# Feeding the first four tiles of a fused attention and MLP kernel in another order: loads on two queues, statistics and norms reordered

## The chip, the cores and the metric

The kernel runs on one core of a Trainium2 chip. The metric is the device time of one execution in microseconds (us). A profile gives the span of one execution, which is about 2 us shorter than its time. Engines are called as in the profile: PE multiplies matrices, PEld is its weight load, DVE is the vector engine, ACT the scalar engine, POOL the general one, SP the one that only issues transfers.

Kernels are compared over five rounds in which the kernel before and the new one run on the same chip.

## The reference, cut to what matters

```python
xn  = layernorm(x)                                # x: 2048 rows of 640, bf16
q, k, v = split(xn @ wqkv)                        # 32 heads of 20
o   = linear_attention(phi(q), phi(k), v) @ wo    # phi = elu + 1
out = x + o + (gelu(xn @ w1 + b1) @ w2 + b2)      # F = 1536
```

The rows are cut into 16 tiles of 128 rows. Tiles 0 to 3 are group 0, tiles 4 to 7 group 1, and so on. Everything begins with four tiles of x: statistics on DVE, the reciprocal root ("rstd") on ACT, the norm on DVE, a transpose on PE, a copy from PSUM to SBUF, and then the product with K's weights.

## The kernel before

PE needs, in this order, tile 0 (only centred, its scale is applied later), then normed tiles 1, 2 and 3. These are the loads and the start of the program, with cuts marked:

```python
load_x(0, 1)                    # SP's queue; 160 KB each tile
load_x(1, 2)
load_x(2, 4)                    # tiles 2 and 3 in one transfer

def emit_later_loads():         # called after the statistics of tile 1
    nc.vector.memset(w1[:, 0, 0:1], 0.0)       # holds w1 back until DVE is there
    nc.sync.dma_start(out=w1[:, :, 0 : F // 2], ...)
    load_x(4, 8)                # group 1
    ...                         # b1, second half of w1, Q's weights, x of groups 2 and 3

nc.vector.memset(wqk[:, 0, D : D + TOK], 0.0)  # holds wk back by 0.27 us
load_wk(0, 3)                   # ACT's queue: K's weights, chunks 0 to 2 (480 KB)
load_wk(3, NC)                  # chunks 3 and 4 (320 KB)
...
emit_stats(0); emit_center(0); emit_T_first(0, ...)      # T: transposes on PE, copies on ACT
emit_warm(1)                    # L190: a matmul of constants, its result isn't used
emit_stats(1)
emit_later_loads()
emit_stats_half(2, 0)
emit_rstd(0, 2)
emit_norm(1)
emit_stats_half(2, 1)
emit_Ka(0, 0, 3)                # first K product, chunks 0 to 2
emit_T_first(1, ((0, 3, nc.scalar.copy),))
emit_rstd(2, 3)
emit_T_first(1, ((3, NC, nc.scalar.copy),))
emit_stats(3)
emit_norm(2)
emit_Ka(0, 3, NC); emit_Kb(0)
emit_Ka(1, 0, 3)
emit_T(2, ...)
emit_rstd(3, 4); emit_norm(3); emit_norm(0)
...                             # K of tiles 1 to 3, then the MLP's first product, L485
```

Of the kernel before, what the change touches and what calls it, by code (L numbers as in the profile page):

```python
# [15 lines left out]
def kernel(  # L16
# [12 lines left out]
    nc = tc.nc  # L29
# [4 lines left out]
    S, D = x2d.shape  # L34
# [4 lines left out]
    NC = D // P  # L39
    NJ = F // P  # L40
    TOK = 512
# [34 lines left out]
    wqk = early.tile([P, NC, 2 * D], BF16, name="wqk", tag="early")  # L76
# [24 lines left out]
    def bank(dtype=F32, hold=False):  # L101
        n = turn.pop(0)
        if isinstance(hold, str):
            named[hold] = n
        else:
            (held if hold else turn).append(n)
        return psum.tile([P, TOK if dtype == F32 else 2 * TOK], dtype, name=f"bank{n}", tag=f"bank{n}")
# [16 lines left out]
    def load_x(t0, t1, queue=nc.sync):  # L124
        queue.dma_start(out=x_all[:, t0:t1, :], in_=xv[:, t0:t1, :])

    def load_wk(k0, k1):
        nc.scalar.dma_start(out=wqk[:, k0:k1, D : 2 * D], in_=wqkv_v[:, k0:k1, D : 2 * D])

    load_x(0, 1)  # L130
    load_x(1, 2)
    load_x(2, 4)

    def emit_later_loads():
        nc.vector.memset(w1[:, 0, 0:1], 0.0)
        nc.sync.dma_start(out=w1[:, :, 0 : F // 2], in_=w1_v[:, :, 0 : F // 2])
        load_x(4, 8)
        nc.sync.dma_start(out=b1_bf[:], in_=B_b1.rearrange("(j p) -> p j", p=P))
        nc.sync.dma_start(out=w1[:, :, F // 2 : F], in_=w1_v[:, :, F // 2 : F])
        nc.sync.dma_start(out=wqk[:, :, 0:D], in_=wqkv_v[:, :, 0:D])  # L140
        load_x(8, 12)
        load_x(12, 16)

    nc.vector.memset(eps_t[:], EPS)
    nc.vector.memset(neg_half[:], -0.5)
    nc.vector.memset(wqk[:, 0, D : D + TOK], 0.0)
    load_wk(0, 3)
    load_wk(3, NC)
    make_identity(nc, identity)

    def emit_masks():
# [45 lines left out]
    def emit_stats_half(t, half):  # L197
        if half == 0:
            stats_of[t] = small.tile([P, 2, nc.vector.BN_STATS_DIM], F32, name="stats")
        st = stats_of[t]  # L200
        nc.vector.bn_stats(out=st[:, half, :], in_=x_all[:, t, half * HALF : (half + 1) * HALF])  # L201
        if half == 1:
            nc.vector.bn_aggr(out=mv[:, t, :], in_=st[:])

    def emit_stats(t):
        emit_stats_half(t, 0)
        emit_stats_half(t, 1)

    def emit_rstd(t0, t1):
        r = rstd[:, t0:t1]  # L210
        nc.scalar.activation(out=r, in_=mv[:, t0:t1, 1], func=ACT.Ln, bias=eps_t[:], scale=1.0)
        nc.scalar.activation(out=r, in_=r, func=ACT.Exp, scale=-0.5)
# [6 lines left out]
    def emit_norm(t, c0=0, c1=NC):  # L219
        ds = slice(c0 * P, c1 * P)  # L220
        nc.vector.tensor_scalar(  # L221
            out=xn[:, t, ds], in0=x_all[:, t, ds], scalar1=mv[:, t, 0:1], scalar2=rstd[:, t : t + 1],
            op0=ALU.subtract, op1=ALU.mult,
        )
# [6 lines left out]
    def emit_T(t, copy, splits=(0, NC)):  # L231
        pT = bank(BF16)[:, 0:D].rearrange("p (c n) -> p c n", n=P)
        for c in range(NC):
            nc.tensor.transpose(pT[:, c, :], xn[:, t, c * P : (c + 1) * P], identity[:])
        for c0, c1 in zip(splits, splits[1:]):
            copy(out=xnT[:, c0:c1, t * P : (t + 1) * P], in_=pT[:, c0:c1, :])
# [15 lines left out]
    def emit_T_first(t, parts):  # L252
        for c0, c1, copy in parts:
            pT = bank()[:, 0 : (c1 - c0) * P].rearrange("p (c n) -> p c n", n=P)
            for c in range(c0, c1):
                nc.tensor.matmul(
                    pT[:, c - c0, :], lhsT=xn[:, t, c * P : (c + 1) * P], rhs=identity[:],
                    start=True, stop=True,
                )
            copy(out=xnT[:, c0:c1, t * P : (t + 1) * P], in_=pT)  # L260
# [45 lines left out]
    def emit_Ka(t, k0=0, k1=NC):  # L306
        if k0 == 0:
            K_ps[t] = bank(hold="first" if t == 0 else t < TPG)
        for k in range(k0, k1):
            nc.tensor.matmul(  # L310
                K_ps[t][:], lhsT=xnT[:, k, t * P : (t + 1) * P], rhs=wqk[:, k, D : D + TOK],
                start=(k == 0), stop=(k == NC - 1),
            )

    def emit_Kb(t):
        g, i = divmod(t, TPG)
        if i == 0:
            rest_ps[g] = bank(hold=True)
        for k in range(NC):
            nc.tensor.matmul(  # L320
                rest_ps[g][:, i * REST : (i + 1) * REST],
                lhsT=xnT[:, k, t * P : (t + 1) * P], rhs=wqk[:, k, D + TOK : 2 * D],
                start=(i == 0 and k == 0), stop=(k == NC - 1), skip_group_check=True,
            )
# [173 lines left out]
    emit_warm(1)  # L498
    emit_stats(1)
    emit_later_loads()  # L500
    emit_stats_half(2, 0)
    emit_rstd(0, 2)
    emit_norm(1)
    emit_stats_half(2, 1)
    emit_Ka(0, 0, 3)
    emit_T_first(1, ((0, 3, nc.scalar.copy),))
    emit_rstd(2, 3)
    emit_T_first(1, ((3, NC, nc.scalar.copy),))
    emit_stats(3)
    emit_norm(2)  # L510
    emit_Ka(0, 3, NC)
    emit_Kb(0)
    emit_Ka(1, 0, 3)
    emit_T(2, nc.vector.tensor_copy, (0, 3, NC))
    emit_rstd(3, 4)
    emit_norm(3)
    emit_norm(0)
# [426 lines left out]
    class Pair:  # L944
# [63 lines left out]
        def copy(self, name):  # L1008
            self.open(name)
            nc.scalar.copy(out=self.ps[name], in_=self.ps["a"])  # L1010
# [219 lines left out]
```

## Time and profile before

| | before |
|---|---|
| time, median of 6 (range) | 197.59 us (197.46 to 197.94) |
| span of the profile | 195.4 us |
| PE busy | 98% of the span |
| statistics of tile 0 start (x0 has landed) | 3.07 us |
| DVE then idle for x2 and x3 | 0.94 us |
| norm 1, norm 2 start | 7.03, 9.01 us |
| first matmul of the MLP | 13.74 us |

From the page of the profile: the span, each engine's busy time with its share, and the shares of the chain of work that ended last.

```profile
span 195.4 us, 3381 instructions
...
PE 190.8 (98%) x1260; PEld 111.8 (57%) x1260; DVE 163.6 (84%) x393; ACT 89.6 (46%) x165; POOL 21.1 (11%) x52
...
PE 93%; DMA 2%; DVE 2%; SPq 0%; issue 0%
```

The chain that ended last, in order of time; columns are start, duration and what ran. "DMA" is a transfer waited for.

```profile
1.72 4.88 DMA x_all<-in_A_x_dram
...
7.03 0.43 DVE xn L221
...
9.10 0.32 DVE xn L221
9.46 0.45 PE bank_201 L234 x5
...
13.90 1.08 PE bank_268 L485 x5
...
192.20 0.29 DVE late L1003
```

The chain runs through the joint load of x2 and x3 (4.88 us from 1.72 to its landing; DVE stood idle for the last 0.94 us of it), then DVE's norms of tiles 1 and 2, then PE alone; the last line is the last DVE addition. From the chain's first matmul of the MLP to that addition everything is PE work until the last few microseconds. So the head, up to about 13.7 us, is where this change can act. (PE's 98% count matmuls of constants too: until 5.27 us most of what PE does is those, L190.)

The timeline of the head (start, duration, engine, line, operation; in brackets the idle time before it and what ended it):

```profile
3.07 0.89 DVE L201 BATCH_NORM_STATS2 stats<-x_all 128x6 f32<-128x320 bf16 x2 [1.81 <-DMA x_all<-in_A_x_dram]
...
6.62 0.49 DVE L201 BATCH_NORM_STATS2 stats<-x_all 128x6 f32<-128x320 bf16 x1 [0.94 <-DMA x_all<-in_A_x_dram]
...
7.03 0.43 DVE L221 TENSOR_SCALAR xn<-x_all,mv,rstd 128x640 bf16<-128x640 bf16 x1
...
9.01 0.39 DVE L221 TENSOR_SCALAR xn<-x_all,mv,rstd 128x640 bf16<-128x640 bf16 x1
...
13.74 1.24 PE L485 MATMUL bank_268<-xnT,w_91 128*128 128x512 bf16 x5
```

The first bracket is x0. The second, 0.94 us, is DVE waiting for the joint load of x2 and x3. Norm 1 stands between the halves of tile 2's statistics, so it comes 0.4 us after that wait ends. L485 is the MLP's first product.

### The profile page before, as it was taken

To read this page: it belongs to the slowest core of one execution; us is meant where nothing else is said; L and a number is where in the kernel's file an instruction comes from. 1 tells how busy PE (TensorE), PEld (TensorE's weight loads), DVE (VectorE), ACT (ScalarE), POOL (GpSimd) and SP (SyncE) were. 2 spreads that over 40 slices of the span, in tenths; PEclk is the share of its full clock that TensorE was granted. 3 is DMA by queue.
4 is the path that set the end of the run, shared out by engine and by line. 5 is a ranking of instruction groups with operands and counts; after the bars stand their busy time and mean duration, and the time that the engine had idled before them with its cause. 6 is when DMAs were issued, how large, how long until landed. Compare 5 with 4: busy or idle time off the path is not lost.

```text
span 195.4 us, 3381 instructions
## 1 busy us (share of the span) xinstructions
PE 190.8 (98%) x1260; PEld 111.8 (57%) x1260; DVE 163.6 (84%) x393; ACT 89.6 (46%) x165; POOL 21.1 (11%) x52
## 2 busy tenths in 40 slices
PE   8999999999999999999999999999999999999993
PEld 2464444544455454443445777767777777777772
DVE  4788969999699998796978989899999999777442
ACT  2559676568679688999795130050011010110100
POOL 1004180003239100002500000000000000000000
PEclk9999999999999999999999999999999999999998
DMA  6999633953443000000009875300201011020113
GB/s 176 311 302 385 241 81 92 325 212 81 127 114 84 0 0 2 0 0 3 0 14 228 301 219 169 105 0 2 70 0 58 13 67 57 12 70 0 67 37 101
DMA packets 24256, 20.15 MB, mean 103 GB/s; under 512 B 11104, under 2 KB 23728, under 8 KB 24240
## 3 DMA queue, kind: packets, MB, share of 16 engines
q1 hardware_dynamic: 23424, 18.95, 31.2%
q10 hardware_dynamic: 816, 0.98, 1.4%
q8 instruction: 10, 0.16, 0.3%
q14 instruction: 6, 0.05, 0.1%
HBM read 12.72 MB, written 5.24 MB: 92 GB/s over the span
## 4 chain that ended last, share of the span: by engine, by line
PE 93%; DMA 2%; DVE 2%; SPq 0%; issue 0%
DMA x_all<-in_A_x_dram 2%; PE bank_1209 L797 2%; PE bank_1282 L826 2%; PE bank_1273 L826 2%; PE bank_2131 L966 1%; PE bank_2047 L966 1%; PE bank_1963 L966 1%; PE bank_1879 L966 1%; PE bank_1790 L966 1%; PE bank_1701 L966 1%; PE bank_1575 L966 1%; PE bank_1433 L966 1%; PE bank_1398 L826 1%; PE bank_1386 L826 1%; PE bank_1529 L966 1%; PE bank_2060 L966 1%
## 5 line engine op out<-in xcount | busy, mean ns | idle before, releaser
L966 PEld LDWEIGHTS <-xn 128*128 128x128 f16 x198 | 19.0, 98 | 7.3 <-issue 0.3
L485 PEld LDWEIGHTS <-w_91 128*128 128x128 bf16 x120 | 11.7, 98 | 13.9
L473 PEld LDWEIGHTS <-wqk 128*128 128x128 bf16 x100 | 9.7, 98 | 11.1
L201 DVE BATCH_NORM_STATS2 stats<-x_all 128x6 f32<-128x320 bf16 x32 | 13.7, 467 | 2.8 <-DMA x_all<-in_A_x_dram 2.8
L310 PEld LDWEIGHTS <-xnT 128*128 128x128 bf16 x80 | 7.2, 98 | 6.3 <-ACT xnT L260 0.5
L826 PEld LDWEIGHTS <-xn 128*128 128x128 bf16 (+1 forms) x80 | 7.8, 98 | 3.0
L221 DVE TENSOR_SCALAR xn<-x_all,mv,rstd 128x640 bf16<-128x640 bf16 x16 | 6.2, 435 | 3.6 <-POOL rstd L217 3.6
L884 DVE TENSOR_TENSOR pqT<-pqT,xnT 128x256 bf16<-128x256 bf16 (+1 forms) x30 | 8.5, 328 | 0.0
L320 PEld LDWEIGHTS <-xnT 128*128 128x128 bf16 x80 | 5.8, 98 | 3.8
L630 PEld LDWEIGHTS <-w_91 128*128 128x128 bf16 (+1 forms) x48 | 4.5, 97 | 5.8 <-issue 0.7
L981 PEld LDWEIGHTS <-Sq 128*128 128x128 f16 x66 | 6.4, 98 | 2.4
L170 POOL TENSOR_SCALAR_AFFINE_SELECT emask<-emask 128x160 int8<-128x160 int8 (+1 forms) x20 | 7.1, 361 | 1.2
L412 DVE TENSOR_TENSOR x_all<-x_all,b2b 128x640 bf16<-128x640 bf16 x16 | 7.0, 480 | 0.0
L271 DVE TENSOR_SCALAR pqT<-pqT 128x512 bf16<-128x512 bf16 x20 | 5.7, 285 | 0.6 <-ACT pqT L268 0.6
L981 PEld LDWEIGHTS <-pqT 128*128 128x128 bf16 x50 | 4.8, 98 | 1.9 <-issue 0.3
L966 PEld LDWEIGHTS <-hT_79 128*128 128x128 bf16 x48 | 4.6, 98 | 1.9
L966 PEld LDWEIGHTS <-hT_80 128*128 128x128 bf16 x48 | 4.7, 98 | 1.7
L1066 ACT CAST late<-bank_1505 128x320 bf16<-128x320 f32 x1 | 0.4, 425 | 10.9 <-PE bank_1509 L1062 10.9
L190 PE MATMUL bank_123<-const-bfloat16-1.0 128*128 128x512 bf16 x10 | 4.4, 626 | 0.8 <-PEq L1214 0.8
L875 DVE TENSOR_TENSOR Sq<-pqT 128x256 f16<-128x256 bf16 x16 | 4.3, 283 | 0.0
L729 DVE TENSOR_TENSOR pk<-pk,GT 128x512 bf16<-128x512 bf16 x10 | 4.2, 421 | 0.0
L630 PEld LDWEIGHTS <-wv 128*128 128x128 f16 x24 | 2.3, 97 | 3.0 <-issue 0.3
(646 smaller groups left out, 510.7 us busy)
## 6 DMA issues: line engine op xcount, KB each, us to landing
xnT<-rec_rows SPq DMA_DIRECT2D x20, 128.0 KB, 2.5
out_dram<-late SPq DMA_DIRECT2D x14, 160.0 KB, 1.8
w_91<-in_B_w_dram SPq DMA_DIRECT2D x2, 960.0 KB, 5.1
x_all<-in_A_x_dram SPq DMA_DIRECT2D x3, 640.0 KB, 6.5
w_93<-in_B_w_dram SPq DMA_DIRECT2D x3, 640.0 KB, 8.1
wqk<-in_A_wqkv_dram SPq DMA_DIRECT2D x1, 800.0 KB, 10.1
wv<-in_A_wqkv_dram SPq DMA_DIRECT2D x1, 800.0 KB
woA<-in_A_wo_dram SPq DMA_DIRECT2D x5, 160.0 KB, 3.2
```

The lines of the kernel that those rows point to most:

```text
L170: nc.gpsimd.affine_select(out=emask[q, block, SKEW - shift : SKEW - shift + H // 4 * DH], in_=emask[q, block, SKEW - shift : SKEW - shift ...
L201: nc.vector.bn_stats(out=st[:, half, :], in_=x_all[:, t, half * HALF : (half + 1) * HALF])
L221: nc.vector.tensor_scalar(out=xn[:, t, ds], in0=x_all[:, t, ds], scalar1=mv[:, t, 0:1], scalar2=rstd[:, t : t + 1], op0=ALU.subtract, op1= ...
L310: nc.tensor.matmul(K_ps[t][:], lhsT=xnT[:, k, t * P : (t + 1) * P], rhs=wqk[:, k, D : D + TOK], start=(k == 0), stop=(k == NC - 1),)
L412: nc.vector.tensor_tensor(out=x_all[:, t, :], in0=x_all[:, t, :], in1=b2b[:], op=ALU.add)
L473: nc.tensor.matmul(ps[:], lhsT=wqk[:, k, m * P : (m + 1) * P], rhs=xnT[:, k, gs], start=(k == 0), stop=(k == NC - 1),)
L485: nc.tensor.matmul(ps[:], lhsT=w1[:, k, j * P : (j + 1) * P], rhs=xnT[:, k, g * TOK : (g + 1) * TOK], start=(k == 0), stop=(k == NC - 1),)
L630: nc.tensor.matmul(self.ps[name][:], lhsT=left[:, c, js], rhs=x_block(*block, c) if block else Tx({4: 3, 5: 0, 6: 1, 7: 2}[p], c), start=( ...
L826: nc.tensor.matmul(ps if len(right.shape) == 3 else ps.rearrange("p (c n) -> p c n", c=NC), lhsT=left[:, t, self.i], rhs=right[:, t], star ...
L884: nc.vector.tensor_tensor(out=pqT[:, c, gs], in0=pqT[:, c, gs], in1=xnT[:, c, gs], op=ALU.mult)
L966: nc.tensor.matmul(self.ps[name][:, cols], lhsT=left[:, j], rhs=right[:, j, cols], start=(start and j == 0), stop=False, skip_group_check= ...
L981: nc.tensor.matmul(self.ps[name][:, cols], lhsT=left[:, c], rhs=right[:, c, cols], start=False, stop=(stop and c == CH - 1), skip_group_ch ...
```

## The change

Its intent is to let PE run without gaps earlier. x2 and x3 become transfers of their own so that x2 needn't wait for x3; x1 goes to ACT's queue ahead of wk so that x2 moves up on SP's; group 1's x also goes to ACT's queue behind wk. Norm 2 moves ahead of the second half of tile 3's statistics; rstd of tile 2 moves ahead of the copies of tile 1; the transposes of tile 2 move ahead of the K product of tile 1.

```diff
     load_x(0, 1)
-    load_x(1, 2)
-    load_x(2, 4)
+    load_x(1, 2, nc.scalar)
+    load_x(2, 3)
+    load_x(3, 4)
 ...
         nc.sync.dma_start(out=w1[:, :, 0 : F // 2], in_=w1_v[:, :, 0 : F // 2])
-        load_x(4, 8)
 ...
-    nc.vector.memset(wqk[:, 0, D : D + TOK], 0.0)
     load_wk(0, 3)
     load_wk(3, NC)
+    load_x(4, 8, nc.scalar)
 ...
     emit_later_loads()
-    emit_stats_half(2, 0)
+    emit_stats(2)
     emit_rstd(0, 2)
     emit_norm(1)
-    emit_stats_half(2, 1)
     emit_Ka(0, 0, 3)
-    emit_T_first(1, ((0, 3, nc.scalar.copy),))
     emit_rstd(2, 3)
-    emit_T_first(1, ((3, NC, nc.scalar.copy),))
-    emit_stats(3)
+    emit_T_first(1, ((0, 3, nc.scalar.copy), (3, NC, nc.scalar.copy)))
+    emit_stats_half(3, 0)
     emit_norm(2)
+    emit_stats_half(3, 1)
     emit_Ka(0, 3, NC)
     emit_Kb(0)
+    emit_T(2, nc.vector.tensor_copy, (0, 3, NC))
     emit_Ka(1, 0, 3)
-    emit_T(2, nc.vector.tensor_copy, (0, 3, NC))
```

## The prediction

> **What bounds it now.** The page's busy shares give PE 98% of a 195.4 us span, and the chain of waits is PE for 93%. Non-PE pieces of the chain lie in the first 9.46 us and in the last 4 us. From 9.46 us on, PE runs without a gap that the change could touch (table of stretches: 100% busy from 9.46 to 60). So the change can only move the moment at which PE becomes dense.
>
> **The head before (timeline, chain).** x0 lands at 3.06. DVE does the statistics of tile 0, centres it, does tile 1 (done 5.66), then sits idle 0.94 us until the joint load of x2 and x3 lands at 6.6: the chain goes through that load for 4.88 us. Statistics of tile 2, first half 6.62, norm 1 at 7.03 to 7.46, both halves of tile 3 (8.02 to 8.85), norm 2 at 9.01 to 9.40; PE transposes tile 2 at 9.46. Between 6.16 and 9.46 PE has about 2.3 us of work (K of tile 0, transposes of tile 1, first three chunks of tile 1): some 1.0 us of idle is all there is to win.
>
> **What the change does.**
> - x2 comes alone and earlier. The order of issue becomes x0, x1 (both at about 0.81, on two queues), x2, wk part 1, x3, wk part 2, x4 to 7. My estimate: x2 at 4.5 to 5, so DVE's 0.94 us wait goes. Wk no longer waits for the memset, but x1 stands ahead: issued at about 1.3 as before. x2 ahead of wk part 1 costs it about 0.4 us at the 400 GB/s measured: 5.4 becomes 5.8, still ahead of its use at 6.16.
> - Worked out with the old durations: statistics 2 at 5.67 to 6.8; rstd of 0 and 1 on ACT at 6.26 to 6.80; norm 1 at 6.85 (was 7.03); half of tile 3; norm 2 at 7.65 to 8.05 (was 9.40). ACT does rstd 2 ahead of both copies of tile 1 (7.7 to 8.5).
> - PE then: transposes 1 at 7.3, K of tile 0 to 8.4, transposes 2 at once, K of tile 1 from 8.7, K of tile 2 from 10.05, transposes 3 at 10.70 (was 11.27 in the chain). Gain 0.57 us, kept to the end.
> - x4 to 7 (640 KB) now go ahead of the first half of w1, which will land at about 11, needed at 13.3: no wait.
>
> **What is taken back.** x0 and x1 are now issued together. The Trainium skill, "DMA: Bandwidth & Descriptors", section "Issuing engines are not separate DMA queues", says that both queues share the same 16 DMA engines and interleave; this trace agrees in that the second wk part (320 KB, issued before 2.3) lands at 7.1. If x1 interleaves with x0, x0 lands up to 0.4 us later, and DVE is then busy from x0 to norm 2, so the delay is paid in full. I take 0.15 us.
>
> **Predicted: 197.15 us** (from 197.59), 8 in 10 between 196.7 and 197.6. Faster by over 2%: 0.01; within 2%: 0.98; slower: 0.01.
>
> **What would show it.** Right: DVE has no wait for x_all after tile 0; norm 2 starts near 7.7; transposes of tile 2 start near 8.4; first MLP product near 13.3; no PE wait for w1. Wrong: statistics of tile 0 start later than 3.3; the first K product waits for wk beyond 6.2; the first MLP product waits for w1; a later non-PE piece in the chain.

## More of the kernel before

"The clock" is the share of full speed that was granted to PE.

A trace records a transfer as pieces (for x and K's weights, single rows of 1280 bytes, or of 5120 bytes where four tiles of x come together) and its landing as 16 parts. A transfer has landed when its last part has.

## The result, and the profile after

The changed kernel takes 197.57 us (median of 10 runs, 197.35 to 197.86), the kernel before, measured beside it, 197.62 us (20 runs, 197.33 to 198.22). The ratio is 0.9992, with a 95% interval of 0.9982 to 1.0003: the same. Ratios here are the mean time of one kernel's runs over that of the other's of the same rounds, so they are not quite the ratio of the medians. Executions over 1.5% slower than the fastest of the same kernel are left out of the means.

The profiled execution took 198.72 us, 1.1 us longer than that median. So its trace can't stand for the timed runs, and this has to be said before reading it. Its page:

```profile
span 196.6 us, 3380 instructions
...
PE 190.8 (97%) x1260; PEld 111.9 (57%) x1260; DVE 163.4 (83%) x392; ACT 89.8 (46%) x165; POOL 21.1 (11%) x52
...
PE 93%; DMA 4%; DVE 1%; SPq 0%; issue 0%
```

Its timeline, the lines that answer to those of before:

```profile
3.94 0.89 DVE L201 BATCH_NORM_STATS2 stats<-x_all 128x6 f32<-128x320 bf16 x2 [2.97 <-DMA x_all<-in_A_x_dram]
...
7.50 0.39 DVE L221 TENSOR_SCALAR xn<-x_all,mv,rstd 128x640 bf16<-128x640 bf16 x1
...
9.12 0.59 PE L310 MATMUL bank_169<-wqk,xnT 128*128 128x512 bf16 x2 [0.72 <-ACT xnT L260]
...
9.27 0.49 DVE L201 BATCH_NORM_STATS2 stats<-x_all 128x6 f32<-128x320 bf16 x1 [1.38 <-DMA x_all<-in_A_x_dram]
...
9.68 0.43 DVE L221 TENSOR_SCALAR xn<-x_all,mv,rstd 128x640 bf16<-128x640 bf16 x1
...
15.09 1.24 PE L485 MATMUL bank_268<-xnT,w_91 128*128 128x512 bf16 x5
```

Statistics of tile 0 start at 3.94 and not at 3.07. The bracket of 0.94 us behind tile 1 is gone, and norm 1 starts at 7.50 (7.03 before). Then x3 comes very late: DVE idles 1.38 us for it, and PE idles 0.72 us ahead of the last two chunks of the first K product. The timeline names ACT's copy for that second wait; but those chunks read tile 0's copy, long done, and the second part of wk landed at 9.09 in this trace, so it was wk. The transfer records show that most of it was there early: of the 16 parts of wk's second transfer 15 had landed by 7.00 and the last at 9.09, of x3's 12 by 6.98 and the last at 9.26. A few parts lagged, the last ones by up to 2.9 us behind the first.

For a trace of the typical run the same kernel was run again (run `a_same` below). It took 197.47 us. Its timeline:

```profile
3.94 0.89 DVE L201 BATCH_NORM_STATS2 stats<-x_all 128x6 f32<-128x320 bf16 x2 [2.97 <-DMA x_all<-in_A_x_dram]
...
7.50 0.39 DVE L221 TENSOR_SCALAR xn<-x_all,mv,rstd 128x640 bf16<-128x640 bf16 x1
...
8.21 0.43 DVE L221 TENSOR_SCALAR xn<-x_all,mv,rstd 128x640 bf16<-128x640 bf16 x1
...
13.86 2.97 PE L485 MATMUL bank<-xnT,w 128*128 128x512 bf16 x13
```

And its chain that ended last:

```profile
0.81 3.11 DMA x_all<-in_A_x_dram
...
7.95 0.45 PE bank L256 x5
...
14.03 6.04 PE bank L485 x28
...
192.32 0.29 DVE late L1002
```

Here DVE waits for x only once, for x0. The chain then goes from x0 straight through DVE (not shown) to the transposes of tile 1, and PE is dense from 7.95 us on (busy for 5.86 of the 5.91 us up to the MLP). Yet the MLP's first matmul starts at 13.86, 0.12 us after that of before (13.74). From that matmul to the last DVE addition it is 192.32 - 13.86 = 178.46 us, and before it is 192.20 - 13.74 = 178.46 us: what follows the head is rigid in both. So the question is only why a head with no gap from 7.95 on isn't earlier than one with gaps. The answer in these lines is the first one, 0.87 us of later start.

### The profile page after: what moved, and what is told of

It reads as the page before. It is cut to its first block, busy times and chain, and to the rows that moved or that the text cites. A ratio compares the mean times of both kernels' runs of the same rounds, so it can differ in the third digit from the quotient of the medians.

```text
span 196.6 us, 3380 instructions
## 1 busy us (share of the span) xinstructions
PE 190.8 (97%) x1260; PEld 111.9 (57%) x1260; DVE 163.4 (83%) x392; ACT 89.8 (46%) x165; POOL 21.1 (11%) x52
## 4 chain that ended last, share of the span: by engine, by line
PE 93%; DMA 4%; DVE 1%; SPq 0%; issue 0%
DMA x_all<-in_A_x_dram 4%; PE bank_1209 L796 2%; PE bank_1273 L825 2%; PE bank_1282 L825 2%; PE bank_2131 L965 1%; PE bank_2047 L965 1%; PE bank_1963 L965 1%; PE bank_1879 L965 1%; PE bank_1790 L965 1%; PE bank_1701 L965 1%; PE bank_1575 L965 1%; PE bank_1433 L965 1%; PE bank_1386 L825 1%; PE bank_1398 L825 1%; PE bank_1529 L965 1%; PE bank_2060 L965 1%
```

## The experiments

Eleven kernels and a repeat were run, in four jobs on four chips, five rounds each. All outputs are right. The last column is where the head ended in the profiled run.

| run | median, range (us) | before in the same job | ratio, 95% interval | statistics 0 start | first MLP matmul |
|---|---|---|---|---|---|
| a_same | 197.47, 197.42 to 197.53 | 197.87 | 0.9983, 0.9967 to 0.9998 | 3.94 | 13.86 |
| x1_back | 198.54, 198.41 to 198.70 | 197.87 | 1.0038, 1.0022 to 1.0054 | 3.31 | 14.49 |
| x4_back | 198.05, 197.38 to 198.78 | 197.87 | 1.0015, 0.9994 to 1.0037 | 3.77 | 13.69 |
| both_back | 197.66, 197.51 to 197.85 | 197.87 | 0.9992, 0.9977 to 1.0007 | 3.25 | 13.85 |
| order_only | 197.90, 197.67 to 198.38 | 197.83 | 1.0010, 0.9990 to 1.0029 | 3.15 | 14.27 |
| loads_only | 197.33, 197.19 to 198.82 | 197.83 | 0.9994, 0.9967 to 1.0022 | 3.79 | 13.72 |
| x2_first | 198.16, 197.48 to 200.46 | 197.83 | 1.0026, 0.9992 to 1.0060 | 3.10 | 14.26 |
| x3_first | 199.56, 198.43 to 200.09 | 197.83 | 1.0086, 1.0061 to 1.0111 | 3.11 | 15.55 |
| x1_late | 197.95, 197.57 to 200.24 | 197.87 | 1.0030, 0.9992 to 1.0068 | 3.15 | 14.00 |
| mixed | 197.93, 197.64 to 198.73 | 197.87 | 1.0006, 0.9985 to 1.0026 | 4.04 | 13.90 |
| x1_act | 198.15, 197.84 to 199.15 | 197.67 | 1.0032, 1.0010 to 1.0054 | 4.04 | 13.97 |
| split3 | 198.00, 197.47 to 198.20 | 197.67 | 1.0011, 0.9992 to 1.0030 | 3.20 | 13.80 |

Theory 1: x1, issued beside x0, makes x0 late, and the new order has no slack to hide it. Theory 2: group 1's x (x4 to 7), queued early, holds x3 and wk back. The lines of the profile below come from the profiled run of each kernel.

### a_same: the change once more

No edit.

> The changed kernel again, for a second trace, since the profiled execution after was 1.1 us longer than the median of the timed ones. Time 197.55 us, within 0.15. Theory 1 (x1 issued beside x0 delays x0, and DVE is busy from x0 on): statistics of tile 0 start at 3.7 to 4.0 in this trace too (3.07 before), and x3 is there by 7. Theory 2 (x4 to 7, queued beside x3 and the second wk part, keep one of the 16 pieces of x3 and wk back): x3 lands again after 8.5. If it is neither, statistics of tile 0 start near 3.1 and x3 lands before 7.

Statistics of tile 0 start at 3.94 again, and x3 landed at 6.23. So x0's lateness is the rule, and the late x3 of the first trace was that execution's own. Its cause wasn't found.

In this job the interval of the change's ratio, 0.9967 to 0.9998, just leaves out 1; in the first it didn't (0.9982 to 1.0003). If the change gains anything, it is under 0.2%, and what differs is the upper end: none of its 15 timed runs in the two jobs took more than 197.86 us, and 13 of the 31 of before did.

### x1_back: x1 again on SP's queue, behind x0

```diff
-    load_x(1, 2, nc.scalar)
+    load_x(1, 2)
 ...
+    nc.vector.memset(wqk[:, 0, D : D + TOK], 0.0)
     load_wk(0, 3)
```

> The change, but x1 again from SyncE's queue after x0, and the memset that holds wk back restored. x4 to 7 stay on ScalarE's queue after wk. Theory 1: statistics of tile 0 start again near 3.1, time about 197.0 us (0.5 faster than the change). Theory 2: no faster than the change, 197.5, since x3 and the second wk part are still late.

Its timeline:

```profile
3.31 0.89 DVE L202 BATCH_NORM_STATS2 stats<-x_all 128x6 f32<-128x320 bf16 x2 [2.05 <-DMA x_all<-in_A_x_dram]
...
8.67 0.49 DVE L202 BATCH_NORM_STATS2 stats<-x_all 128x6 f32<-128x320 bf16 x1 [1.31 <-DMA x_all<-in_A_x_dram]
```

x0 is back to 3.3, as Theory 1 says; but the time rose to 198.54, in all of its runs, and that neither theory had forecast. x3's wait is why: 1.31 us. As the fourth transfer on SP's queue x3 is now issued at 2.2, and x4 to 7 at 2.3. The parts of x3 landed between 6.81 and 8.66. The Trainium skill, "DMA: Bandwidth & Descriptors", section "Queues, rings and completion order", says that each transfer engine takes turns between the queues it has work for, packet by packet. The sizes fit: a piece of x3 is 1280 bytes (55 ns, median in the trace), a piece of x4 to 7 is 5120 bytes (204 ns). Eight pieces of x3 for each engine, each behind a large one, are 8 x (55 + 204) = 2.1 us by my estimate, if a turn is a single piece, and 1.85 us were measured. The records fit turns of about one piece: from 6.4 to 7.2 us, 44 pieces of x3 and 52 of x4 to 7 started. The test is both_back below, which differs from this kernel only in that x4 to 7 come late: there x3's parts landed within 0.63 us (6.77 to 7.40), and the median, in the same job, is 0.88 us lower. So Theory 2's mechanism is real, but in this kernel and not in the change, where x3 is issued 0.5 us ahead of x4 to 7.

### x4_back: x4 to 7 again late, on SP's queue

```diff
         nc.sync.dma_start(out=w1[:, :, 0 : F // 2], ...)
+        load_x(4, 8)
 ...
-    load_x(4, 8, nc.scalar)
```

> The change, but x4 to 7 again on SyncE's queue after the first half of w1; x1 stays on ScalarE's queue ahead of wk. Theory 1: no change, 197.5 us, statistics of tile 0 still start at 3.7 to 4.0. Theory 2: x3 and wk land by 7, time about 197.1 us.

x0 stays late (3.77), x3 lands at 6.14, and the head ends at 13.69, about where it ends in a_same. The median is 0.6 us above that of a_same, with one run as fast (197.38, the profiled one) and one at 198.78. Theory 2 falls as the taker of the gain. But a_same and this kernel differ only in x4 to 7 and ran in the same job on one chip, so these 0.6 us (medians of five runs and six) are what issuing x4 to 7 early is worth in the change. What it seems to protect is seen under x1_act.

### both_back: four x transfers on SP, x4 to 7 late, the new order

Both edits above together.

> Both undone: x0 to x3 as four transfers on SyncE's queue, wk held by the memset, x4 to 7 after the first half of w1; the new order of the statistics, norms and transposes stays. Theory 1: 197.0 us, as x1_back. Theory 2: 197.1 us, as x4_back. If both play a part: faster than each alone, down to 196.9. If splitting and reordering are worth nothing: 197.6.

```profile
3.25 0.89 DVE L202 BATCH_NORM_STATS2 stats<-x_all 128x6 f32<-128x320 bf16 x2 [1.99 <-DMA x_all<-in_A_x_dram]
...
6.44 0.89 DVE L202 BATCH_NORM_STATS2 stats<-x_all 128x6 f32<-128x320 bf16 x2 [0.59 <-DMA x_all<-in_A_x_dram]
```

x0 is at 3.25, but now x2 is awaited for 0.59 us: with x1 back on SP's queue, x2 is issued at 1.7, after the first part of wk (1.3), and lands at 6.43. The wait moved from x0 to x2, and the head ends at 13.85. Time as before.

### order_only: the old loads, the new order

> The old loads with the new order of statistics, norms, rstd and transposes. Theory 1 (the new order pays only if x2 is there early; x0's delay is what the loads cost): x2 and x3 land together at 6.6 as before, norm 1 now stands behind both halves of tile 2 and starts at about 7.6 (7.03 before), so it is slower than before by 0.2 to 0.3 us. Rival (the order alone is worth the forecast 0.57): faster than before by 0.4 or more.

```profile
6.86 0.89 DVE L201 BATCH_NORM_STATS2 stats<-x_all 128x6 f32<-128x320 bf16 x2 [1.10 <-DMA x_all<-in_A_x_dram]
...
7.91 0.39 DVE L221 TENSOR_SCALAR xn<-x_all,mv,rstd 128x640 bf16<-128x640 bf16 x1
```

With x2 and x3 at 6.85, norm 1 now stands behind both halves of tile 2: 7.91 for 7.03. The head ends at 14.27, 0.53 us later than before (0.24 us of it is the landing, 6.86 for 6.62). The forecast direction shows in the trace; in the time it is not clear (1.0010, the interval holds 1). The order alone gains nothing.

### loads_only: the new loads, the old order

> The new loads with the old order. Theory 1: statistics of tile 0 start at 3.8 to 4.0, and the 0.94 us wait for x2 that stood behind tile 1 is gone, so norm 1 starts near 7.0 and norm 2 near 9.0, both as before: time as before within 0.15. Rival (x0's delay is paid in full in any order): slower than before by 0.5 or more.

```profile
3.79 0.89 DVE L201 BATCH_NORM_STATS2 stats<-x_all 128x6 f32<-128x320 bf16 x2 [2.82 <-DMA x_all<-in_A_x_dram]
...
6.99 0.45 DVE L221 TENSOR_SCALAR xn<-x_all,mv,rstd 128x640 bf16<-128x640 bf16 x1 [0.20 <-ACT rstd L212]
...
8.99 0.39 DVE L221 TENSOR_SCALAR xn<-x_all,mv,rstd 128x640 bf16<-128x640 bf16 x1
```

x0 is at 3.79 and nothing else is awaited. Norm 1 and norm 2 start at 6.99 and 8.99, against 7.03 and 9.01 before. In the old order the late x0 is paid out of the wait for x2 that was there anyway: 0.72 us late at the first statistics, not late at all at norm 1. Four of six runs lie at 197.19 to 197.41, two at 197.97 and 198.82, so the mean is no better than before.

### x2_first: x0 alone at the start, x2 ahead of wk

As both_back, and a longer memset, so that wk is issued after x2:

```diff
-    nc.vector.memset(wqk[:, 0, D : D + TOK], 0.0)
+    nc.vector.memset(wqk[:, 0:3, D : D + TOK], 0.0)
```

> x0 to x3 as four transfers on SyncE's queue, wk held back by a longer memset (0.8 us for 0.27) until x2 has been issued, x4 to 7 late as before, the new order. So x0 has no rival at the start, and x2 stands ahead of wk. Theory 1: statistics of tile 0 start at 3.1 to 3.3, no wait of DVE for x2 (it lands by 5.0), norm 1 near 6.9, the first MLP product near 13.3 in the chain: 197.0 us, 0.5 to 0.7 faster than before. If pieces of x2 land late here too: as both_back, 197.6.

What PE waited for (total, times, longest):

```profile
PE bank L311 <- DMA wqk<-in_A_wqkv_dram: 1.5, 1, 1.5
```

Everything on DVE came as forecast: statistics at 3.10, no wait for x2 (though it landed at 5.70, just in time, and not by 5.0), norm 1 at 6.84. But the first part of wk, issued at 1.83 (1.29 in both_back), landed at 7.68, and PE waited 1.5 us for it. The wait moved to wk. The head ends at 14.26, and the time is not below before.

### x3_first: all four x transfers ahead of wk

As x1_back (x4 to 7 on ACT's queue), with the memset over all five chunks of wk, 1.3 us.

> As x1_back (x4 to 7 on ScalarE's queue behind wk), but wk and with it x4 to 7 held by a memset of 1.3 us until x3 too has been issued. If x1_back was slow because x3 shared the rings with the larger pieces of x4 to 7 (x3 at 8.66 there), x3 lands here by 6 and the time falls from 198.5 to 197.0 to 197.3; wk's first part then lands near 6.2, which may cost the first K product up to 0.2. If x1_back was slow for another reason, it stays near 198.5.

It was slower still, 199.56 us. Here x3 landed at 6.22 and was never awaited, which fits the reading of x1_back (wk was moved too, so both_back is the cleaner test). But wk's first part, issued only at 2.36, came at 7.32. PE waited 1.95 us, and something followed. Three stretches; the columns are the stretch, its length, busy time of PE, PEld, DVE, ACT and POOL (with instructions), the granted clock, the share of the transfer engines and GB/s:

```profile
4.39:7.80 3.41, 1.46 (x12) 0.65 (x10) 3.34 (x12) 2.42 (x7) 0.00 (x0) 1.00 1.04 359
7.80:11.22 3.42, 3.42 (x21) 2.29 (x20) 0.97 (x5) 1.72 (x5) 0.00 (x0) 0.50 1.03 363
11.22:14.00 2.78, 2.73 (x26) 1.71 (x25) 1.52 (x7) 0.37 (x1) 0.20 (x1) 1.00 1.05 213
```

PE was busy for 1.46 us of the stretch of 3.41 us that holds the wait, and in the next 3.42 us the clock was at 0.50. That is a second cost of letting PE starve, on top of the wait. In the traces of x2_first and x1_late, with waits of 1.5 and 1.2 us, the clock stayed at 1.00; PE was busy for 1.93 and 2.19 us of the 3.41 us that hold them (6.20 to 9.61, 6.24 to 9.65).

The timed runs tell what it costs. This trace's mean clock is 0.991, and so is that of five of x3_first's six runs (199.41 to 200.09 us); the sixth has 1.000 and took 198.43. That is 1.0 to 1.7 us, from one run against five. The longest runs of other kernels have 0.991 too: two of x2_first (199.73, 200.46) and of x1_late (199.26, 200.24), one of x1_act (199.15), and one of before (199.64).

### x1_late: the change, with x1 issued after x0

```diff
+    nc.vector.memset(x_all[:, 1, 0:TOK], 0.0)
+    load_x(1, 2, nc.scalar)
     load_wk(0, 3)
```

(and the early `load_x(1, 2, nc.scalar)` taken away).

> The change with one thing added: a 0.27 us memset of x1's place on DVE, so that ScalarE issues x1 at about 1.3 and not at 0.8, after x0's issue is done; wk and x4 to 7 follow it. All else as the change. If x0's lateness comes from x1 being issued beside it, statistics of tile 0 start at 3.1 to 3.3 (3.77 to 3.94 in the traces with x1 beside x0). If also x2 lands by 5.6 and the first wk part by 6.3, the forecast's own sequence comes true: norm 1 near 6.9, first MLP product starts at 13.0 to 13.3 (13.86 in the second trace of the change), 196.8 to 197.1 us. If DMA pieces lag as in x2_first, a wait of PE for wk or of DVE for x2 takes it back and the median is 197.5 or more. Rival (x0 is late for the order of the program or the missing memset on wk, not for x1): statistics of tile 0 start at 3.8 again.

```profile
3.15 0.89 DVE L202 BATCH_NORM_STATS2 stats<-x_all 128x6 f32<-128x320 bf16 x2 [1.89 <-DMA x_all<-in_A_x_dram]
...
7.46 0.81 PE L311 MATMUL bank<-wqk,xnT 128*128 128x512 bf16 x3 [1.23 <-ACT rstd L212]
```

x0 is at 3.15. The edit moves x1 (issued at 1.29 for 0.80) and with it what follows on ACT's queue (wk at 1.70 for 1.22, then x4 to 7); x1_act below, where wk stays at 1.29, settles that it is x1. x1 landed at 4.93, and DVE waited 0.23 us for it. And wk was late again. PE's first K product waited 1.23 us, until 7.46; the profile names ACT's rstd, on which this product doesn't depend, while the transfer that landed at 7.43, just ahead, was the first part of wk. The forecast sequence didn't come true. The head ends at 14.00.

### mixed: the new loads, the old order, and only norm 2 moved up

```diff
 (loads_only)
-    emit_stats(3)
+    emit_stats_half(3, 0)
     emit_norm(2)
+    emit_stats_half(3, 1)
```

> The new loads, the old order of the PE work, norm 1 again between the halves of tile 2, and of the new order only the split of tile 3's statistics around norm 2. Theory: norm 1 stays at 7.0 as in loads_only, norm 2 starts at about 8.8 for 8.99, set by rstd of tile 2 on ScalarE, and the first MLP product starts at about 13.5 (13.72 in loads_only): 197.1 to 197.2 us, 0.15 to 0.3 under before. If norm 2 isn't what holds PE, no difference from loads_only (197.3).

Inconclusive: in this trace x0 was at 4.04 and x3 was awaited 0.26 us, so norm 2 came at 9.07. What is of use is another wait of PE:

```profile
PE bank L310 <- DMA xnT<-xn_rows: 0.5, 1, 0.5
```

This is the K product of tile 4 at 33.8 us, waiting for the last transposed chunk of group 1. So the part behind the head isn't rigid without limit.

### x1_act: the kernel before with one line changed

```diff
-    load_x(1, 2)
+    load_x(1, 2, nc.scalar)
```

> The kernel before with one line changed: x1 from ScalarE's queue, so issued beside x0. Everything else old. Theory 1: this alone makes x0 late: statistics of tile 0 start at 3.75 to 4.05 (3.06 to 3.31 in all traces where x1 is issued after x0). The old order has a wait for x2 and x3 behind tile 1, which takes most of the delay up: norm 1 starts at 7.0 to 7.2 and the first MLP product at 13.7 to 13.9, time as before within 0.2 us. Rival: statistics of tile 0 at 3.1 to 3.3, or the delay paid in full, 0.6 us or more slower.

The head of its timeline:

```profile
4.04 0.89 DVE L201 BATCH_NORM_STATS2 stats<-x_all 128x6 f32<-128x320 bf16 x2 [2.78 <-DMA x_all<-in_A_x_dram]
...
7.24 0.45 DVE L221 TENSOR_SCALAR xn<-x_all,mv,rstd 128x640 bf16<-128x640 bf16 x1 [0.20 <-ACT rstd L212]
```

This is the disputed cost by itself. One line moves the statistics of tile 0 from 3.07 to 4.04. Norm 1 comes at 7.24, so 0.97 us have shrunk to 0.21, and the head ends at 13.97. But the ratio is 1.0032, about 0.6 us (0.48 by the medians), and I had said within 0.2. Two later lines of the timeline show where more is lost:

```profile
13.98 0.89 DVE L201 BATCH_NORM_STATS2 stats<-x_all 128x6 f32<-128x320 bf16 x2 [0.28 <-DMA x_all<-in_A_x_dram]
...
33.47 0.10 PEld L310 LDWEIGHTS <-xnT 128*128 128x128 bf16 x1 [0.62 <-DMA xnT<-xn_rows]
```

w1 is held back until the statistics of tile 1 are done, so a late x0 makes w1 late too (issued at 6.68 and not 5.71), and x4 to 7 behind it (landed at 13.97; 12.69 before). Group 1's statistics wait 0.28 us, its norms and its transposed x come later, and at 33.47 the K product of tile 4 has waited for the last chunk. From the first MLP matmul to the last addition it is 192.73 - 13.97 = 178.76 us, 0.30 us more than elsewhere. The weight loads at that place in the kernel before have no wait, all five chunks go in a row:

```profile
31.87 0.96 PEld L310 LDWEIGHTS <-xnT 128*128 128x128 bf16 x5
```

How narrow it is shows when all traces are compared. From the start of group 1's transposing transfers to the first of these loads it is 7.43 us before (24.44 to 31.87). All nine traces with 7.43 us or more have no wait. All five with less do: x1_late (7.31 us, last load delayed by 0.21), split3 (7.06, 0.62), x4_back (6.72, 0.42), x1_act (6.69, 0.62) and mixed (6.46, 1.03). From the first MLP matmul to the end they lose 0.00, 0.30, 0.09, 0.30 and 0.71 us. With the early x4 to 7 they start at 23.79 in a_same and 24.25 in loads_only (in mixed at 25.57 and in x1_late at 24.83, so that isn't all that moves them). I read the early x4 to 7 as what keeps x0's delay from reaching group 1 through w1's hold: the two kernels with a late x0 and a late x4 to 7, x4_back and x1_act, have medians of 198.05 and 198.15, and those with a late x0 and an early x4 to 7 and nothing else changed, a_same and loads_only, 197.47 and 197.33. a_same and x4_back ran side by side, the other two on other chips, so the first pair is a test and the second is support. It also fits that a_same's and the change's timed runs never exceeded 197.86, while those of before reach 198.22 and 198.31 in the same jobs; but slow executions of before were not traced, and both_back, with x4 to 7 as late as before, never exceeded 197.85 either, so that is argued, not shown.

### split3: the kernel before, only norm 2 moved up

The edit of mixed, on the kernel before.

> The kernel before with its own loads, only norm 2 put ahead of the second half of tile 3's statistics. Theory: norm 2 moves from 9.01 to about 8.8, held then by rstd of tile 2 on ScalarE, and the first MLP product starts about 0.15 to 0.2 earlier: 0.1 to 0.2 us faster than before, if x2 and x3 land at 6.6 as in the trace of before. If DMA pieces land late, nothing is to be seen in the median.

Norm 2 started at 8.97, held by rstd of tile 2 on ACT as expected, 0.04 us earlier than before although x2 had come 0.13 us later. The transposes of tile 2 started at 9.47 as before: PE had only just finished the K chunks of tile 1 that stand ahead of them. No gain, and 0.30 us lost at tile 4 (192.56 - 13.80 = 178.76). Nothing in the median.

### What was not settled

No variant beat the change and the kernel before clearly: the lowest median, loads_only's, has an interval of its ratio that holds 1. All eight traces in which x0 is issued alone have x0 at 3.07 to 3.31. The six in which x1 is issued beside it have 3.77 to 4.04. The first MLP matmul, however, never came before 13.69, because wherever x0 was early, x2, x3 or wk was late instead. A count of the pieces of these first transfers shows a difference that I hadn't expected: of the 896 to 1,152 pieces of 1280 bytes in the first 8 us (55 ns each in the median), 25 to 35 took over 200 ns where x0 is issued alone, and 10 to 18 where x1 is beside it. Why a piece stalls, and why single transfer engines then lag by 1 to 3 us, stays open.

## Why the prediction was right, and where its sizes were off

The time lies in the range (197.57, range 196.7 to 197.6), at its upper edge, and "within 2%" was right. This is luck more than insight: the range reached up to where a change without any effect would land, and of the forecast gain of 0.44 us (197.59 to 197.15) 0.05 us were measured (197.62 to 197.57), less than the noise. The steps were right, one size was not. Point by point:

- "The change can only move the moment at which PE becomes dense": right. From the first MLP matmul to the last addition it is 178.46 us before and after. It has a limit that I didn't name: group 1 must be back from its transposing transfers by the K product of tile 4. Three traces (x1_act, split3, mixed) lost 0.3 to 0.7 us between the first MLP matmul and the end, and all three show that wait. So "x4 to 7 now go ahead of w1", for which I forecast only that it does no harm, was worth 0.6 us by the medians of a_same and x4_back.
- "DVE's 0.94 us wait goes" and "x2 at 4.5 to 5": right; x2 landed at 4.46, the first wk part at 5.79 (forecast 5.8), x4 to 7 at 8.67 (a_same).
- "PE then: ...": the sequence was right. Forecast were transposes of tile 3 at 10.70 in the chain, measured was 11.40. The gain of 0.57 us turned into a loss of 0.12 us at the first matmul of the MLP.
- "I take 0.15 us", with a ceiling of 0.4, for x0 landing later: this is the term that was mis-sized. It measured 0.87 us (0.70 to 0.97 in the six traces with x1 beside x0). Between 0.57 - 0.15 = 0.42 us of forecast gain and 0.12 us of loss lie 0.54 us, and this term was 0.87 - 0.15 = 0.72 us too small; 0.22 us came back because norm 1 follows the first statistics after 3.56 us and not after 3.78 as I had worked out.
- The ceiling came from 160 KB at the 400 GB/s of the full stream. The stretches of the kernel before show that x0 doesn't move at that rate (last column, GB/s):

```profile
2.00:2.50 0.50, 0.50 (x2) 0.15 (x1) 0.00 (x0) 0.22 (x1) 0.00 (x0) 1.00 0.77 236
2.50:3.00 0.50, 0.50 (x3) 0.21 (x2) 0.00 (x0) 0.50 (x1) 0.00 (x0) 1.00 1.21 187
...
4.50:5.00 0.50, 0.50 (x2) 0.11 (x1) 0.50 (x3) 0.00 (x0) 0.00 (x0) 1.00 1.12 425
```

At 187 GB/s 160 KB (163,840 bytes) take 0.88 us, at 236 GB/s 0.69 us (estimates from these lines, picked after the result), and the delays were 0.70 to 0.97. The transfer records show two things behind it. First, the two queues alternate: the 128th piece on SP's queue (x0 has 128) ended at 2.66 us before and at 3.33 in a_same, and by then 110 pieces had ended on ACT's queue, none before. Second, the pair starts more slowly than x0 alone: by 2.50 us 69 to 98 pieces had ended in the eight traces with x0 alone, and 19 to 43, of both queues together, in the six with x1 beside it. Sharing doesn't explain that, and its cause stays open. x1 beside x0 also gains what x0 loses: x1 landed at 4.15 in a_same, before at 4.30, with x0 at 3.94 and 3.06. The pair is done at about the same time; only, the program needs x0 first.
- "DVE is then busy from x0 to norm 2, so the delay is paid in full": right, and this is the heart of it. In the old order (loads_only) the same delay costs nothing at norm 1. In the new order it costs all of itself: x3_first, in the same order with x0 at 3.11 and no wait for x1 to x3, has norms 1 and 2 at 6.67 and 7.38, and a_same, with x0 0.83 us later, has them at 7.50 and 8.21, 0.83 us later each. The change spent the slack that would have hidden its own side effect.

## What to carry to other kernels

A second queue doesn't add a lane at the start: a transfer issued beside the one that everything waits for takes its share of a stream that isn't yet at full rate (and here made that stream start more slowly), so size that delay with the rate of those microseconds and not with the rate of the full stream. When a change removes a wait, ask what that wait was hiding: here 0.9 us of idle DVE would have hidden the later x0, and the new order had removed it. And look for the next deadline behind the stage that you speed up; here it is group 1's way through DRAM, with next to nothing to spare (7.43 us before, and a first wait at 7.31).

## What the Trainium skill lacked or had wrong

- "DMA: Bandwidth & Descriptors", section "Issuing engines are not separate DMA queues", says that the queues share the same transfer engines and interleave. The runs agree, and show the cost that it doesn't name: a 160 KB transfer issued at the same moment from the other queue made the first one land 0.7 to 1.0 us later (x1_act 4.04 for 3.07; a_same 3.94).
- The same page gives a first-byte latency and rates by size of transfer, but no rate for the first transfers of a kernel. In the kernel before, the first 2 us of traffic (1.5 to 3.5 us) ran at 38 to 236 GB/s, and then it was about 400; in a_same, with x1 beside x0, it was 20 and 84 GB/s up to 2.5 us and then 302 and more. And single pieces of 1280 bytes, 55 ns in the median, took up to 1.05 us (x3_first).
- The same page, section "Queues, rings and completion order", describes turns by packet. A consequence is missing: a transfer with small pieces loses to one with large pieces on the other queue (x1_back: x3 with 1280-byte pieces was spread over 1.85 us beside 5120-byte pieces, over 0.63 us without them in both_back).
- "TensorE: Matmul & The Clock Gate", Part 1, has the clock fall to half after at least one idle window of about 3.4 us. In x3_first the clock was at 0.50 for 3.41 us after a window of 3.41 us that wasn't idle: PE was busy for 1.46 us of it, and its longest wait was 1.95 us. With 1.93 and 2.19 us busy (x2_first, x1_late) the clock stayed at 1.00. The page names frequent short gaps as well, further down, but not how busy is busy enough.
